# A first weight load issued in two parts, and the activations loaded as half rows, in a two-model decode attention kernel

## The chip, the cores and the metric

The kernel runs on one core of a Trainium2 chip. The metric is the device time of one execution in microseconds, the median of several runs. Profiles are of one execution, on the same core; its span runs from the first to the last instruction.

## The reference

Two independent attention blocks, A and B, each decode one token for 8 sequences. Each has its own x, K cache, V cache, wq and wo, and the two outputs are put side by side.

```python
B, Sq, D = 8, 1, 1024
H, Sk, Dh = 32, 4096, 128
q = (x @ wq).reshape(B, Sq, H, Dh).transpose(0, 2, 1, 3)
scores = einsum("bhqd,bhkd->bhqk", q, k_cache) * Dh ** -0.5
p = softmax(scores, axis=-1)
o = einsum("bhqk,bhkd->bhqd", p, v_cache)
out = o.transpose(0, 2, 1, 3).reshape(B, Sq, H * Dh) @ wo
```

All tensors are bf16. With one query per sequence, each byte of the caches is used once: K and V of both blocks, wq and wo come to 1,107 MB that must be read.

## The kernel before

**Tiles.** K and V are cut into tiles of one sequence and eight heads: 128 partitions (8 heads by 16 stretches of the key positions) of 64 KB each. There are 32 K tiles and 32 V tiles for each block, 64 pairs in all, numbered n = 0 to 63 (A first). The two wq and the two wo have the size of one such tile too.

**The ring.** All of them pass through `ring`, three slots of 64 KB on each partition (line 166). The `plan` (lines 237 to 241) fixes the order and the slot: wq of A into slot 1, K0 into slot 0, wq of B into slot 2, then K(n+1) into the slots 0 and 1 by turns and V(n) into slot 2. At the end come wo of A and of B. A load is issued when the last reader of the slot's tenant before is done (`load_tiles`, lines 257 to 275); `opUse` holds that last reader. Every load of the plan is issued by SyncE, in the plan's order, on SyncE's queue (queue 1 of the profile), so a load that waits holds up those behind it. Slot 2 has x as its first tenant (line 239): both x lie there (line 440) until they are transposed, so wq of B waits for the transposes.

**The x loads.** The two x (8 rows of 1,024 values, 2 KB a row) are issued by ScalarE on its own queue (queue 10), after `c_oh`, an early step on VectorE (line 441). `emit_xT` (lines 443 to 449) transposes them on PE: 16 transposes of 8 x 128 into PSUM tile `misc`, seen as bf16. VectorE copies them to `xT` (line 452). A column group of `xT` is 8 sequences of one of 8 chunks of D; the chunk k holds the rows p * 8 + k of wq, since wq is laid out with 8 consecutive rows on each partition.

**The q projection.** `make_q(c)` (lines 278 to 293) multiplies `xT` with wq of block c, 64 matmuls of 512 columns in two halves, and ScalarE copies the result to SBUF (L291). `make_qT` transposes it (L301 on PE, L305 on VectorE). `make_stage` (L312, ScalarE) and `make_qbc` (L317 PE, L319 ScalarE) spread the eight heads' q over the 128 partitions of a tile as `qbc`.

**The stages.** For each n, K tile n is worked in four chunks: VectorE multiplies with `qbc` (L330), adds halves (L335), PE adds up further in PSUM with identity matmuls (L345), VectorE reduces the rest (L353). Softmax's maximum, exponent and masks follow (L359 to L370); P times V of tile n - 1 runs on PE (L382) during the stage of tile n. Block B's q projection stands in tile 0's stage on PE, between the third and the fourth chunk's L345 (lines 471 to 474), and frees slot 2 for V0.

**The end.** After the last tile the sums are normalised and the wo products are made (L431). The output of each block is stored by SyncE (line 436); the store's DRAM side is written `"b (q n) -> q b n"` with q = 4, its SBUF side has 32 rows.

**Order of issue.** `P.run` writes each engine's instructions out in the order in which they were added, with a semaphore wait before an instruction where needed. SyncE's first two loads are issued ahead of the block in which the engines run side by side (line 507), the rest in it (line 512).

Of the kernel before, what the change touches and what calls it, by code (L numbers as in the profile page):

```python
# [31 lines left out]
class _Program:  # L32
# [11 lines left out]
    def add(self, eng, emit, deps=(), dma_key=None, moves=False):  # L44
        op = _Op(eng, emit, list(deps), dma_key, moves)
        if dma_key is not None:
            self.counts[dma_key] = self.counts.get(dma_key, 0) + 16
            op.token = (dma_key, self.counts[dma_key])
        for d in op.deps:
            if not (d.eng == "pe" and eng == "pe"):  # L50
                d.sig = True
        self.ops[eng].append(op)
        return op
# [86 lines left out]
def _build_kernel(nc, caches, out):  # L140
    B, Sq, D = caches[0][0].shape
    _, H, Sk, Dh = caches[0][1].shape
    NC = len(caches)
    assert B == 8 and Sq == 1 and Dh == 128 and Sk == 4096 and D == 1024 and H % 8 == 0 and 128 % H == 0
    DC = D // 128
# [16 lines left out]
    with es:  # L162
# [3 lines left out]
        ring = sb("ring", [128, 3, T * Dh], BF16)  # L166
        ident = sb("ident", [128, 128], BF16)
# [4 lines left out]
        xT = sb("xT", [128, NC * DC * B], BF16)  # L172
# [20 lines left out]
        misc = ps("misc")  # L193
        proj = ps("proj")
        q_ps = [o_ps, pv_ps]
        misc_bf16 = misc.bitcast(BF16)

        wo_cuts = ((0, 20), (20, H - 4), (H - 4, H - 1), (H - 1, H))
        sems = {e: es.enter_context(nc.semaphore(f"c_{e}")) for e in ENGINES[1:]}
# [4 lines left out]
        P = _Program()  # L204
        add = P.add

        def dma(out_ap, in_ap, key, deps, eng="sp"):
            return add(eng, lambda e: e.dma_start(out_ap, in_ap), deps, dma_key=key)
# [16 lines left out]
        c_oh = add("dve", lambda e: e.tensor_copy(own_h[:], own), [c_own])  # L225
# [5 lines left out]
        opT, opMul, opEacc, opRed, opNgm, opExp = {}, {}, {}, {}, {}, {}  # L231
# [18 lines left out]
        def where(n):  # L250

            return n // (B * HB), n // HB % B, n % HB

        def tile_of(kind, n):
            return ring[:, slot[(kind, n)], :]

        def load_tiles():
            while issued[0] < len(plan):
                kind, n, w = plan[issued[0]]
                prev = before[issued[0]]  # L260
                dep = opUse.get(prev)
                if prev is not None and dep is None:
                    return
                to, key = ring[:, w, :], ("t", w)
                if kind in ("k", "v"):
                    c, b, hb = where(n)
                    from_ = caches[c][1 if kind == "k" else 2][b, hb * HQ:(hb + 1) * HQ].rearrange("u (m t) d -> (u m) (t d)", m=MP)
                    opT[(kind, n)] = dma(to, from_, key, [dep])
                elif kind == "wq":
                    opT[(kind, n)] = dma(to[:, 0:DC * H * Dh], caches[n][3].rearrange("(p k) n -> p (k n)", k=DC), key, [dep])  # L270
                else:
                    from_ = caches[n][4].rearrange("(p r) n -> p (r n)", r=H)
                    for i, (r0, r1) in enumerate(wo_cuts if n == NC - 1 else ((0, H),)):
                        opT[(kind, n, i)] = dma(to[:, r0 * D:r1 * D], from_[:, r0 * D:r1 * D], key if n < NC - 1 else ("w", i), [dep])
                issued[0] += 1


        def make_q(c):
            w = tile_of("wq", c)
            for f in range(2):  # L280
                def emit(e, f=f):
                    for k in range(DC):
                        for hb in range(HB):
                            col = k * H * Dh + (2 * hb + f) * 512
                            i = e.matmul(q_ps[f][32 * hb:32 * hb + B, :], xT[:, (c * DC + k) * B:(c * DC + k + 1) * B],  # L285
                                         w[:, col:col + 512], start=(k == 0), stop=(k == DC - 1), tile_position=(0, 32 * hb))
                    return i
                opQ[(c, f)] = add("pe", emit, [c_xT, opT[("wq", c)]] + [opQs.get((c - 1, hb, f)) for hb in range(HB)])
                for hb in range(HB):
                    rows = slice(32 * hb, 32 * hb + B)  # L290
                    opQs[(c, hb, f)] = add("act", lambda e, rows=rows, f=f: e.activation(q_sb[rows, c, f * 512:(f + 1) * 512], q_ps[f][rows, :], ACTF.Copy),  # L291
                                           [opQ[(c, f)]])
            opUse[("wq", c)] = opQ[(c, 1)]
# [143 lines left out]
                            ("out", 0), [opEv[c]] if c == NC - 1 else [opEv[c], opT[("wo", NC - 1, len(wo_cuts) - 2)]], "sp"))  # L437


        x_sb = ring[0:B, 2, 0:NC * D].rearrange("p (c d) -> p c d", c=NC)  # L440
        op_x = [dma(x_sb[:, c, :], caches[c][0].rearrange("b s d -> b (s d)"), ("x", 0), [c_oh], "act") for c in range(NC)]

        def emit_xT(e):
            for c in range(NC):
                for k in range(DC):
                    col = (c * DC + k) * B
                    i = e.transpose(misc_bf16[:, col:col + B], x_sb[:, c, :].rearrange("b (p k) -> b k p", k=DC)[:, k, :],
                                    ident[0:B, 0:B])
            return i
        op_xT = opUse[("x", 0)] = add("pe", emit_xT, [c_ident, op_x[-1]])  # L450
        load_tiles()
        c_xT = add("dve", lambda e: e.tensor_copy(xT[:], misc_bf16[:, 0:NC * DC * B]), [op_xT])
        make_q(0)
        make_qT(0)
        make_stage(0)
# [3 lines left out]
        for n in range(NQ):  # L459
            P.mark(n)  # L460
            for r in range(NR):
                s = n * NR + r
                make_mul(s)
                if s >= LAG:
                    make_red(s - LAG)
                if r == LAG - 1 and n >= 1:
                    make_shift(n - 1)
                fold = make_fold(s)
                if r == LAG - 1 and n >= 1:
                    make_pm(n - 1)  # L470
                if n == 0 and r == NR - 1:
                    for c in range(1, NC):
                        make_q(c)
                        make_qT(c)
                if r == 2 and n >= 1:
                    make_pv(n - 1, 0, RG // 2)
                if r == 3 and n >= 1:
                    make_pv(n - 1, RG // 2, RG)
                    make_acc(n - 1)
                if r == 2 and n + 1 < NQ:  # L480
                    make_stage(n + 1)
                    make_qbc(n + 1)
                make_eacc(s, fold)
                load_tiles()
                if r == 3 and n >= 1:
                    make_ext(n - 1)
        P.mark(NQ)
        n = NQ - 1
# [4 lines left out]
        make_pv(n, 0, RG)  # L493
        make_acc(n)
        load_tiles()
        make_ext(n)
        make_norm(1)
# [6 lines left out]
            o.token = (("x", 0), 16 * NC)  # L504
        loops = {"pe": (1, 2, (NQ - 2) // 2), "dve": (3, 2, (NQ - 4) // 2), "act": (3, HB, (NQ - 4) // HB)}

        P.run("sp", nc.sync, sems, part=(0, 2))
        with nc.Block() as block:

            @block.sync  # L510
            def _(eng):
                P.run("sp", eng, sems, part=(2, None))

            @block.tensor
            def _(eng):
                P.run("pe", eng, sems, loops["pe"])

            @block.scalar
            def _(eng):
                P.run("act", eng, sems, loops["act"])  # L520

            @block.vector
            def _(eng):
                P.run("dve", eng, sems, loops["dve"])

            @block.gpsimd
            def _(eng):
                P.run("pool", eng, sems)
# [4 lines left out]
def bass_concat_heads__mha_block_cached__mha_block_cached__decode_kernel(  # L533
    nc, A_x, A_k_cache, A_v_cache, A_wq, A_wo, B_x, B_k_cache, B_v_cache, B_wq, B_wo, out,
):
    caches = [(A_x, A_k_cache, A_v_cache, A_wq, A_wo), (B_x, B_k_cache, B_v_cache, B_wq, B_wo)]
    _build_kernel(nc, caches, out)
# [28 lines left out]
```

## Time and profile before

| what | value |
|---|---|
| median of 3 runs | 2563.64 us (2563.33 to 2563.65) |
| span of the profiled execution | 2562.3 us |
| PE busy | 1115.7 us, 44% |
| VectorE (DVE) busy | 2170.6 us, 85% |
| ScalarE (ACT) busy | 129.9 us, 5% |
| queue 1 (SyncE's loads), share of 16 DMA engines | 99.9% |
| read from HBM | 1107.33 MB |

The median of the runs is 1.3 us above the profiled span, which leaves out what lies before the first and after the last instruction.

How to read the rows. A row of the timeline gives start, duration, engine, line, operation, the tile written and the tile read, and in brackets how long the engine was idle before and what ended that. PE is TensorE, DVE VectorE, ACT ScalarE, SP SyncE; a name with q (SPq, ACTq) is the engine's sequencer, which issues DMAs. A row of a DMA view gives packets, megabytes and the share of 16 DMA engines. A packet is one row of a transfer, or the 4-byte signal with which a DMA engine reports its part done; "under 512 B" counts such signals, and "under 2 KB" and "under 8 KB" include them. A view may be cut to a stretch of time; its 40 slices then divide that stretch. Packets are booked where they start.

### The profile page before, as it was taken

The numbers are of one execution on the slowest core, as the hardware profiler recorded it, in microseconds if no ns is written. First come the engines' busy times: TensorE is split into PE (matmuls) and PEld (weight loads), VectorE is DVE, ScalarE is ACT, GpSimd is POOL, SyncE is SP. The second block draws the span as 40 slices with busy tenths as digits, with TensorE's granted clock in tenths as the row PEclk, the third lists the DMA queues.
The fourth block names the chain that finished last, engine by engine and source line by source line (L and its number), as shares of the span: only waits on it lengthen the run. The fifth ranks groups of instructions, "written<-read, shape, count | busy, mean of one in ns | idle before, by whom it ended". The sixth has DMA issues, their size and how long they took to land.

```text
span 2562.3 us, 18832 instructions
## 1 busy us (share of the span) xinstructions
PE 1115.7 (44%) x7712; PEld 396.7 (15%) x7712; DVE 2170.6 (85%) x1042; ACT 129.9 (5%) x401; POOL 2.6 (0%) x15
## 2 busy tenths in 40 slices
PE   2443443443443443444444444434444434434434
PEld 1111111111111111111111111111111111111112
DVE  3898898898898898898898888988988988988983
ACT  1100000000000000000000000000000000000000
POOL 0000000000000000000000000000000000000000
PEclk7676766767767767766666766767667666767667
DMA  9999999999999999999999999999999999999999
GB/s 425 427 438 430 437 431 436 432 436 432 435 431 437 430 438 430 435 432 435 433 431 437 431 435 433 434 433 435 433 435 433 435 433 435 433 435 433 435 433 394
DMA packets 19554, 1107.51 MB, mean 432 GB/s; under 512 B 2184, under 2 KB 2248, under 8 KB 2520
## 3 DMA queue, kind: packets, MB, share of 16 engines
q1 hardware_dynamic: 19512, 1107.34, 99.9%
q8 instruction: 7, 0.11, 0.0%
q10 hardware_dynamic: 32, 0.03, 0.0%
q14 instruction: 3, 0.02, 0.0%
HBM read 1107.33 MB, written 0.03 MB: 432 GB/s over the span
## 4 chain that ended last, share of the span: by engine, by line
DMA 52%; DVE 28%; issue 16%; PE 4%; ACT 0%; another core or an unknown queue 0%; DVEq 0%; SPq 0%
DMA ring<-in_A_k_cache_dram 25%; DMA ring<-in_B_k_cache_dram 25%; DVE ring L330 10%; DVE ring L335 10%; PE red L345 4%; DVE s_sb L353 4%; DVE PM L370 3%; DMA ring<-in_B_wo_dram 2%; DVE rmax L359 1%; DVE rtmp L360 0%; ACT PM L291 0%; DVEq L135 0%; DVE ngm L363 0%; PE o L285 0%
## 5 line engine op out<-in xcount | busy, mean ns | idle before, releaser
L330 DVE TENSOR_TENSOR ring<-ring,qbc 128x8192 bf16<-128x8192 bf16 x256 | 1131.7, 4421 | 310.9 <-DMA ring<-in_A_k_cache_dram 158.0
L345 PE MATMUL red<-ring,ident 128*128 128x512 bf16 x2048 | 780.1, 550 | 1392.7 <-DVE ring L335 1392.7
L335 DVE TENSOR_TENSOR ring<-ring 128x4096 bf16<-128x4096 bf16 x256 | 582.3, 2274 | 0.0
L345 PEld LDWEIGHTS red<-ring,ident 128*128 128x128 bf16 x2048 | 238.5, 127 | 1842.6 <-DVE ring L335 1495.2
L353 DVE TENSOR_REDUCE s_sb<-red 128x64 f32<-128x1024 f32 x256 | 312.0, 1219 | 2.9 <-PE red L345 2.9
L382 PE MATMUL pv<-ring,PM 128*32 128x512 bf16 x4096 | 274.4, 415 | 4.6 <-DVE PM L370 4.6
L370 DVE TENSOR_TENSOR PM<-pe,own_h 128x2048 bf16<-128x2048 bf16 x64 | 146.2, 2284 | 0.7 <-ACT pe L365 0.7
L382 PEld LDWEIGHTS pv<-ring,PM 128*32 128x32 bf16 x4096 | 103.9, 104 | 188.4 <-issue 116.2
L319 ACT ACTIVATE qbc<-misc 128x128 bf16<-128x128 f32 x64 | 17.8, 278 | 1093.4 <-PE misc L317 1093.4
L365 ACT ACTIVATE pe<-s_sb,ngm 128x256 bf16<-128x256 f32 x64 | 32.5, 508 | 470.2 <-DVE ngm L363 470.2
L390 ACT ACTIVATE accS<-pv 128x512 bf16<-128x512 f32 x64 | 38.2, 597 | 350.5 <-PE pv L382 350.5
L399 PEld LDWEIGHTS o<-accS,E 128*32 128x32 bf16 x1024 | 31.3, 100 | 49.3 <-issue 48.1
L399 PE MATMUL o<-accS,E 128*32 128x32 bf16 x1024 | 38.1, 185 | 0.7 <-ACT accS L390 0.7
L405 ACT ACTIVATE o_sb<-o 32x32 f32 (+1 forms) x64 | 11.9, 186 | 449.5 <-PE o L399 448.9
L359 DVE TENSOR_REDUCE rmax<-s_sb 128x1 f32<-128x256 f32 x64 | 26.9, 420 | 2.2
L435 DVE CAST orow<-proj 128x256 bf16<-128x256 f32 x2 | 0.8, 424 | 28.7 <-PE proj L431 28.7
L431 PE MATMUL proj<-ring,on_sb 128*32 128x256 bf16 x256 | 12.1, 363 | 17.7 <-DMA ring<-in_A_wo_dram 9.9
L312 ACT ACTIVATE qst<-qT 128x128 bf16 (+1 forms) x64 | 18.7, 293 | 2.0 <-DVE qT L305 2.0
L305 DVE COPY qT<-misc 128x64 bf16<-128x64 bf16 x8 | 3.5, 436 | 17.6 <-PE misc L301 17.6
L360 DVE TENSOR_SCALAR rtmp<-half,rmax 128x32 f32<-128x32 f32 x64 | 15.4, 241 | 2.2
L363 DVE TRANSPOSE_TENSOR_REDUCE ngm<-rtmp 128x1 f32<-128x32 f32 x64 | 13.5, 211 | 2.2
L317 PE MATMUL misc<-ident,qst 128*128 128x128 bf16 x64 | 14.8, 232 | 0.9 <-ACT qst L312 0.9
(33 smaller groups left out, 65.5 us busy)
## 6 DMA issues: line engine op xcount, KB each, us to landing
ring<-in_B_wo_dram SPq DMA_DIRECT2D x1, 5120.0 KB, 33.6
ring<-in_B_wo_dram SPq DMA_DIRECT2D x1, 2048.0 KB, 38.2
ring<-in_B_wo_dram SPq DMA_DIRECT2D x1, 768.0 KB, 39.6
ring<-in_A_k_cache_dram SPq DMA_DIRECT2D x32, 40.0
ring<-in_A_v_cache_dram SPq DMA_DIRECT2D x32, 27.8
ring<-in_B_k_cache_dram SPq DMA_DIRECT2D x32, 39.8
ring<-in_B_v_cache_dram SPq DMA_DIRECT2D x32, 27.8
ring<-in_B_wo_dram SPq DMA_DIRECT2D x1, 256.0 KB, 39.7
```

Source lines behind the costliest of these rows:

```text
L312: return e.activation(qst[:, n % 2, :].rearrange("p (j m) -> p j m", m=MP), from_.unsqueeze(2).to_broadcast([128, HQ, MP]), ACTF.Copy)
L319: opQbc[n] = add("act", lambda e: e.activation(qbc[:, n % 2, :], misc[:, 0:Dh], ACTF.Copy), [opQb[n], _at(opMul, NR * (n - 2) + NR - 1)])
L330: opMul[s] = add("dve", lambda e: e.tensor_tensor(v, v, qbc[:, n % 2, :].unsqueeze(1).to_broadcast([128, CT, Dh]), ALU.mult), [opT[("k", n ...
L335: return add("dve", lambda e: e.tensor_tensor(v[:, :, 0:64], v[:, :, 0:64], v[:, :, 64:128], ALU.add), [opMul[s]])
L345: i = e.matmul(dst, ident[:], v[:, g, :, j, :], start=(j == 0), stop=(j == 3))
L353: opRed[s] = add("dve", lambda e: e.tensor_reduce(s_sb[:, n % 2, r * CT:(r + 1) * CT], red_ps[s % 2][:, :].rearrange("p (t w) -> p t w", w ...
L359: m = add("dve", lambda e: e.tensor_reduce(rmax[:], s_sb[:, n % 2, :], AX.X, ALU.max), [opRed[NR * n + NR - 1]])
L365: opExp[n] = add("act", lambda e, at: e.activation(pe[:], s_sb[:, n % 2, :], ACTF.Exp, bias=ngm[:, n % 2:n % 2 + 1], scale=scale, accum_ou ...
L370: opPM[n] = add("dve", lambda e: e.tensor_tensor(PM[:], pe[:].unsqueeze(2).to_broadcast([128, T, HQ]), own_h[:].unsqueeze(1).to_broadcast( ...
L382: i = e.matmul(pv_ps[32 * q:32 * (q + 1), :], PM[:, t:t + 4, :].rearrange("p t j -> p (t j)"), v[:, t * Dh:(t + 4) * Dh], start=(g == 0), ...
L390: opAcc[n] = add("act", lambda e: e.activation(accS[:], pv_ps[:], ACTF.Copy), [opPV[n], _at(opExt, n - 1)])
L399: x = e.matmul(to, E[:, i, PH - 1 - u:PH - 1 - u + MB], accS[:, i * 128 + H * u:i * 128 + H * (u + 1)], start=(i == 0 and u == 0), stop=(i ...
```

## The change

Three things are changed, and two follow from them.

1. The first load, wq of A, is issued as two DMAs: rows 0 to 15, then rows 16 to 127. Both count on the semaphore of slot 1; the q projection waits for the second's count. Three loads instead of two are now issued ahead of the block.
2. Each x is loaded as 16 half rows of 512 values: half 0 of the 8 sequences on 8 partitions, half 1 on the next 8. The two x take 32 partitions, the destination of each is 16 rows of 1 KB. The source is written with the half outermost.
3. The transposes become matmuls. For each chunk k and each half h, the 32 half rows (64 values of the chunk in each) are multiplied by the 16 columns of the identity that belong to that half; the result, 64 partitions by 16 columns (A's sequences, then B's), goes to partitions 64 h to 64 h + 63 of `misc`. There are 16 of these, with f32 results.
4. `xT` has the chunk outermost and the block inside it, and `make_q` reads it so.
5. The copy to `xT` reads `misc` as f32.

```diff
@@ load_tiles
                 elif kind == "wq":
-                    opT[(kind, n)] = dma(to[:, 0:DC * H * Dh], caches[n][3].rearrange("(p k) n -> p (k n)", k=DC), key, [dep])
+                    from_ = caches[n][3].rearrange("(p k) n -> p (k n)", k=DC)
+                    for p0, p1 in ((0, 16), (16, 128)) if n == 0 else ((0, 128),):
+                        opT[(kind, n)] = dma(to[p0:p1, 0:DC * H * Dh], from_[p0:p1, :], key, [dep])
@@ make_q
-                            i = e.matmul(q_ps[f][32 * hb:32 * hb + B, :], xT[:, (c * DC + k) * B:(c * DC + k + 1) * B],
+                            i = e.matmul(q_ps[f][32 * hb:32 * hb + B, :], xT[:, (k * NC + c) * B:(k * NC + c + 1) * B],
@@ after make_proj
-        x_sb = ring[0:B, 2, 0:NC * D].rearrange("p (c d) -> p c d", c=NC)
-        op_x = [dma(x_sb[:, c, :], caches[c][0].rearrange("b s d -> b (s d)"), ("x", 0), [c_oh], "act") for c in range(NC)]
+        x_sb = ring[0:NC * 2 * B, 2, 0:D // 2]
+        op_x = [dma(x_sb[2 * B * c:2 * B * (c + 1), :], caches[c][0].rearrange("b s (h e) -> h (b s) e", h=2), ("x", 0), [c_oh], "act")
+                for c in range(NC)]
 
         def emit_xT(e):
-            for c in range(NC):
-                for k in range(DC):
-                    col = (c * DC + k) * B
-                    i = e.transpose(misc_bf16[:, col:col + B], x_sb[:, c, :].rearrange("b (p k) -> b k p", k=DC)[:, k, :],
-                                    ident[0:B, 0:B])
+            mine = ident[0:2 * NC * B, 0:2 * NC * B].rearrange("p (c h b) -> p h c b", c=NC, h=2)
+            for k in range(DC):
+                for h in range(2):
+                    i = e.matmul(misc[64 * h:64 * (h + 1), k * NC * B:(k + 1) * NC * B].rearrange("p (c b) -> p c b", c=NC),
+                                 x_sb.rearrange("b (p k) -> b k p", k=DC)[:, k, :], mine[:, h], start=True, stop=True, tile_position=(0, 64 * h))
             return i
...
-        c_xT = add("dve", lambda e: e.tensor_copy(xT[:], misc_bf16[:, 0:NC * DC * B]), [op_xT])
+        c_xT = add("dve", lambda e: e.tensor_copy(xT[:], misc[:, 0:NC * DC * B]), [op_xT])
@@ the loads ahead of the block
-        P.run("sp", nc.sync, sems, part=(0, 2))
+        P.run("sp", nc.sync, sems, part=(0, 3))
...
-                P.run("sp", eng, sems, part=(2, None))
+                P.run("sp", eng, sems, part=(3, None))
```

## The prediction

> **What bounds the kernel now.** I read the page first, the mean rate and the row of DMA queues, to see which resource is never idle.
>
> ```profile
> span 2562.3 us, 18832 instructions
> DMA packets 19554, 1107.51 MB, mean 432 GB/s; under 512 B 2184, under 2 KB 2248, under 8 KB 2520
> q1 hardware_dynamic: 19512, 1107.34, 99.9%
> q10 hardware_dynamic: 32, 0.03, 0.0%
> ```
>
> Queue 1 is SyncE's. It keeps all 16 DMA engines at work for 99.9% of the span, at 432 GB/s. So the time is the bytes at that rate plus a start and an end; nothing done on a compute engine counts unless it makes queue 1 run dry. One 64 KB row on each of the 16 DMA engines is 1.049 MB, and at 432 GB/s takes 2.43 us (2.42 us below). A tile of 128 rows is eight such rows per DMA engine, 19.4 us. Queue 10 is ScalarE's: only the two x loads.
>
> Then the start, in order of time, for what SyncE issues and what each issue has waited for.
>
> ```profile
> 0.80 0.39 SPq L208 DMA_DIRECT2D ring<-in_A_wq_dram  x1
> 1.26 0.41 SPq L208 DMA_DIRECT2D ring<-in_A_k_cache_dram  x1
> 2.49 0.60 ACTq L208 DMA_DIRECT2D ring<-in_A_x_dram  x1
> 3.12 0.28 ACTq L208 DMA_DIRECT2D ring<-in_B_x_dram  x1
> 15.75 1.10 PE L447 MATMUL misc<-ident,ring 8*128 8x8 bf16 x16 [15.75 <-DMA ring<-in_B_x_dram]
> 16.89 0.33 SPq L208 DMA_DIRECT2D ring<-in_B_wq_dram  x1
> 16.89 0.23 DVE L452 COPY xT<-misc 128x128 bf16<-128x128 bf16 x1 [14.17 <-PE misc L447]
> 23.03 3.59 PE L285 MATMUL o<-ring,xT 128*8 128x512 bf16 x32 [6.17 <-DMA ring<-in_A_wq_dram]
> 29.25 0.33 SPq L208 DMA_DIRECT2D ring<-in_A_k_cache_dram  x1
> 34.33 0.28 ACT L319 ACTIVATE qbc<-misc 128x128 bf16<-128x128 f32 x1 [0.38 <-PE misc L317]
> 43.48 4.43 DVE L330 TENSOR_TENSOR ring<-ring,qbc 128x8192 bf16<-128x8192 bf16 x1 [9.87 <-DMA ring<-in_A_k_cache_dram]
> 72.76 0.33 SPq L208 DMA_DIRECT2D ring<-in_A_v_cache_dram  x1
> 80.93 0.33 SPq L208 DMA_DIRECT2D ring<-in_A_k_cache_dram  x1
> 82.18 4.42 DVE L330 TENSOR_TENSOR ring<-ring,qbc 128x8192 bf16<-128x8192 bf16 x1 [4.32 <-DMA ring<-in_A_k_cache_dram]
> ```
>
> SyncE issues in order: wq of A, K0, then wq of B, which waits until the transposes (L447) have freed ring slot 2, then K1, V0, K2. Until wq of B is issued, queue 1 holds just two tiles, 16 rows per DMA engine. **Everything hangs on when x lands**: now shortly before the transposes start at 15.75, with wq of B issued at 16.89, while those 16 rows last until about 41 us. The q projection then starts at 23.03, when wq of A is there, not when x is; its result (qbc) is ready at 34.61, 8.87 us before VectorE gets K0. So x has slack now. The question is whether the new x load keeps it.
>
> **How a small load gets through.** The packets in five stretches, one row time each after the first, in order: 0 to 7.2, 7.2 to 9.7, 9.7 to 12.1, 12.1 to 14.6 and 14.6 to 15.72 us.
>
> ```profile
> q1 hardware_dynamic: 32, 2.10, 77.0%
> ...
> DMA packets 24, 1.06 MB, mean 426 GB/s; under 512 B 0, under 2 KB 0, under 8 KB 8
> q10 hardware_dynamic: 8, 0.02, 1.7%
> ...
> DMA packets 24, 1.05 MB, mean 437 GB/s; under 512 B 8, under 2 KB 8, under 8 KB 8
> q10 hardware_dynamic: 8, 0.00, 0.2%
> ...
> DMA packets 24, 1.06 MB, mean 426 GB/s; under 512 B 0, under 2 KB 0, under 8 KB 8
> ...
> DMA packets 24, 1.05 MB, mean 936 GB/s; under 512 B 8, under 2 KB 8, under 8 KB 8
> ```
>
> In each of the last four, the DMA engines start 16 rows of queue 1 and 8 packets of queue 10: x of A (8 packets of 2 KB), its signals (8 packets under 512 B), x of B, its signals. All four were issued by 3.40 us, yet no two went back to back: **each packet of queue 10, even a 4-byte signal, waits for a 64 KB row of queue 1.** One turn costs 2.42 us. Today an x load of 8 rows has one row and one signal on each of 8 DMA engines, so both x take 4 turns.
>
> Over how many DMA engines is a load spread? The stretch 2560.2 to 2561.2 holds one output store, of 32 rows of 512 B; that from 15.72 to 41 us holds the signals of wq of A.
>
> ```profile
> DMA packets 36, 0.02 MB, mean 16 GB/s; under 512 B 4, under 2 KB 36, under 8 KB 36
> ...
> DMA packets 177, 10.50 MB, mean 415 GB/s; under 512 B 16, under 2 KB 16, under 8 KB 16
> ```
>
> A 128-row tile ends in 16 signals, x in 8, and the store in 4, though its SBUF side has 32 rows: its DRAM side is written "q b n" with q = 4 outermost. The spread follows the smaller outermost count.
>
> **The change, part by part.**
>
> *x over two DMA engines.* The new source is "h (b s) e" with h = 2 outermost, since the halves can't be merged with the rows; the destination has 16 rows. As with the store I take 2 DMA engines, each with 8 rows of 1 KB and a signal, so 9 packets per x and 18 for both, where there were 4. The other bound is 16 DMA engines, by the destination's rows, again 4 turns. The store is the same shape of access, so I take 2. [...]
>
> *When x lands then.* With a row between any two, 18 packets from about 7.3 us would need until 7.3 + 17 x 2.42 = 48.4 us. But queue 1 has only 16 rows per DMA engine: when they are gone the rest goes at once. The first rows of queue 1 start at about 1.9 us and end at about 5.1:
>
> ```profile
> GB/s 0 0 0 0 0 0 0 0 0 0 3641 1820 0 0 364 0 0 0 0 0 0 0 0 0 0 0 364 2185 1092 2185 0 0 0 0 0 0 0 0 0 0
> ```
>
> (the 40 slices of 0 to 7.2 us; bytes are booked where a packet starts, so the second rows start at 4.7 to 5.4). The 16th row ends at 5.1 + 15 x 2.42 = 41.4 us, plus 16 x rows at 0.04 us each (1 KB at the 27 GB/s of one DMA engine): x lands at **42.1 us**. Whether signals of queue 1 take a turn, or x begins one row earlier, doesn't move this; the end of queue 1 sets it.
>
> *First gap.* From the last signals (they stand in the stretch from 14.6 on) to PE's start at 15.75 are at most 1.15 us; I take the middle, 0.6. The transposes to the issue take 1.14 (15.75 to 16.89): wq of B is issued at 43.85. From an issue on idle DMA engines to the end of the first row were 4.3 us at the start (0.80 to 5.1). So wq of B's first row ends at 48.15, where it would have ended at 41.4 + 2.42 = 43.85 without a pause: **4.3 us lost**. If the restart takes 1.0 us plus a plain row of 2.42 (first bytes came 1.0 us after the first issue), it is 3.4.
>
> *Second gap.* xT is copied by 44.1 and the q projection starts at 44.15. From its start to qbc are 11.58 us (23.03 to 34.61), so VectorE starts K0 at 55.75, not 43.48: **12.3 us late**. V0 needs wq of B's slot, freed by B's q projection, which stands on PE behind three chunks of K0: it is issued at 72.76 + 12.3 = 85.05, and its first row ends at 89.35. Queue 1 with wq of B and K1 is dry at 48.15 + 15 x 2.42 = 84.45. V0's first row would have ended at 5.1 + 32 x 2.42 + 0.1 for the old x = 82.65 before. The two gaps together: 89.35 - 82.65 = **6.7 us**, 2.4 of it the second.
>
> *After that.* VectorE starts K1 at 82.18 - 4.32 + 12.3 = 90.2, 8.0 us late. The next V and K:
>
> ```profile
> 112.27 0.33 SPq L208 DMA_DIRECT2D ring<-in_A_v_cache_dram  x1
> 119.01 0.33 SPq L208 DMA_DIRECT2D ring<-in_A_k_cache_dram  x1
> 120.87 4.43 DVE L330 TENSOR_TENSOR ring<-ring,qbc 128x8192 bf16<-128x8192 bf16 x1 [4.78 <-DMA ring<-in_A_k_cache_dram]
> ```
>
> V1 is issued at about 120.3; queue 1 holds V0 and K2 until 89.35 + 15 x 2.42 = 125.7. Covered by 4 us after the restart's 1.0. VectorE is done with K1 at 116.09 + 8.0 = 124.1, before K2 lands, so it is back in step with the DMA, and the stages behind keep their margins.
>
> *The rest.* The load in 16 and 112 rows has one row and then seven per DMA engine, the same bytes: 16 signals more, of 4 bytes each, and one issue more on SyncE, 0.46 us ahead of K0, hidden by the 19 us of wq of A in the queue. The first row may start earlier because fewer rows are prepared (a gain of up to 0.3 us), or the second part may come late for it (a loss of as much): I take nothing. The 16 matmuls now contract 32 rows into 64 columns; the nearest row is the old 1.10 us, with 0.8 to 1.6 as bounds. The copy reads f32: the old 0.23 us to the mean of the final copies, twice as wide; I take 0.25.
>
> ```profile
> L435 DVE CAST orow<-proj 128x256 bf16<-128x256 f32 x2 | 0.8, 424 | 28.7 <-PE proj L431 28.7
> ```
>
> Both are on the path behind x, so ±0.5 us goes into the range. xT's new order of columns changes no instruction of the projection.
>
> **Sum.** I take 6.5 us, a little below 6.7 since the restart may be the shorter one. Span 2562.3 + 6.5 = 2568.8; the runs stand 1.3 us above the span (2563.64): **2570.1 us**, 0.25% slower.
>
> **The rivals.**
>
> *x lands early, nothing changes: 2563.5 us, chance 0.12.* Either x is spread over 16 DMA engines, or the 8 rows of one x share a turn. For the latter: no row of this trace has several small rows of one load beside a busy queue 1. Against it: a row and its signal, and the signal and the next x, never shared a turn. It decides from the number of turns: x must land by about 36 us (the K0 multiply may slip some 6 us before V0's issue comes after queue 1's end), so 12 turns or fewer. Then the time is that of before, less at most 0.3 us for the balance of the DMA engines, the not slower side. [...]
>
> *Only the first gap: 2567.5 us (3.4 to 4.3 lost), chance 0.06.* If the q chain runs faster from a late start, V0 comes in time. Nothing in the rows between 23.03 and 34.61 is waiting for DMA, so I give it little.
>
> *A third gap: 2573 to 2577 us, chance 0.04.* V1's margin is only 4 us. If VectorE runs later than reckoned, PV of tile 0 comes late and V1 leaves queue 1 dry too, each us late costing one, plus the restart.
>
> *Really faster, chance 0.02.* Queue 1 is at 99.9% now: there is no pause to remove, apart from 1 us at the start.
>
> **How the numbers follow.** The forecast has 0.76: 2568.8 to 2571.5 us. A difference under 0.2% (5.1 us) can't be told from none. Slower: 0.76 + 0.04 = 0.80. Same: 0.12 + 0.06 = 0.18. Faster: 0.02. The range 2566.5 to 2573.5 holds the forecast, the single gap and the low end of the third, and leaves out the early x.
>
> **What would show it.** Right: queue 10 with 32 rows and 4 signals (36 packets), spread from about 5 to 42 us; the transposes near 42.7; wq of B issued near 43.9; a hole in the DMA row between 41 and 45 and one near 85; the first K0 multiply near 55.8; VectorE waiting for K2 as before. Wrong: x landed by 20 us, or 16 signals per x, or a hole but no later V0.

## The result, and the profile after

The changed kernel takes 2590.85 us (median of 4 runs, 2590.32 to 2592.92); the kernel before took 2563.51 us beside it. The ratio is 1.0108, 95% interval 1.0096 to 1.012: 27.3 us slower, where 6.5 were forecast.

The head of the page and its rows of DMA queues:

```profile
span 2589.9 us, 18863 instructions
GB/s 271 396 435 435 436 429 433 435 436 432 429 436 435 435 426 435 435 436 431 432 433 437 431 431 435 435 433 429 435 435 435 430 434 433 436 432 431 435 435 394
q1 hardware_dynamic: 19528, 1107.34, 99.6%
q10 hardware_dynamic: 36, 0.03, 0.0%
```

The loss lies in the first two slices (65 us each): 271 and 396 GB/s, then 426 to 437 and a last slice of 394, as before. Queue 10 has 36 packets: 32 rows of x and 4 signals, so each x did go over two DMA engines. But the gap that was forecast for the first slice, 4.3 us of 65, can't bring it down to 271. The timeline of the start:

```profile
0.80 0.87 SPq L208 DMA_DIRECT2D ring<-in_A_wq_dram  x2
62.22 1.12 PE L450 MATMUL misc<-ident,ring 32*64 32x16 bf16 x16 [62.22 <-DMA ring<-in_B_x_dram]
63.37 0.35 SPq L208 DMA_DIRECT2D ring<-in_B_wq_dram  x1
63.73 3.58 PE L287 MATMUL o<-ring,xT 128*8 128x512 bf16 x32 [0.38 <-DVE xT L455]
75.71 4.42 DVE L332 TENSOR_TENSOR ring<-ring,qbc 128x8192 bf16<-128x8192 bf16 x1 [1.11 <-ACT qbc L321]
106.16 0.33 SPq L208 DMA_DIRECT2D ring<-in_A_v_cache_dram  x1
148.85 4.42 DVE L332 TENSOR_TENSOR ring<-ring,qbc 128x8192 bf16<-128x8192 bf16 x1 [3.88 <-DMA ring<-in_A_k_cache_dram]
```

The chain is the forecast one (transposes, then wq of B, then the q projection, then K0, then V0), but the transposes start at 62.22, not near 42.7. The table of stretches says why. A line gives a stretch and its length, the busy time of PE, of PE's weight loads, of VectorE, ScalarE and GpSimd with the number of instructions, the granted clock of PE, and in the last two columns the share of the 16 DMA engines and the rate in GB/s (a packet is booked where it starts, so a share can pass 1). First come two lines of the kernel before, for its first 64 KB row on each DMA engine and for eight later ones:

```profile
1.82:4.85 3.03, 0.00 (x0) 0.00 (x0) 0.41 (x3) 1.28 (x1) 1.68 (x8) 1.00 1.08 368
21.90:41.20 19.30, 7.84 (x97) 3.28 (x97) 1.74 (x4) 5.49 (x11) 0.00 (x0) 0.75 1.01 435
```

and these are of the changed kernel, for its first part of wq of A, its second, K0, and the two gaps:

```profile
1.85:11.20 9.35, 0.00 (x0) 0.00 (x0) 0.41 (x3) 1.28 (x1) 1.64 (x8) 1.00 1.47 217
11.20:41.00 29.80, 0.00 (x0) 0.00 (x0) 0.00 (x0) 0.00 (x0) 0.00 (x0) 1.00 0.89 227
41.00:60.50 19.50, 0.00 (x0) 0.00 (x0) 0.00 (x0) 0.00 (x0) 0.00 (x0) 1.00 0.95 404
60.50:65.00 4.50, 2.40 (x32) 1.48 (x36) 0.29 (x1) 0.00 (x0) 0.00 (x0) 1.00 0.67 234
103.00:108.00 5.00, 3.46 (x60) 1.36 (x52) 2.55 (x3) 3.44 (x6) 0.00 (x0) 0.93 0.62 210
```

Both gaps are there, near 62 and near 105. What the forecast did not have is the first 41 us. The DMA engines are busy all that time (0.89 and more), yet move half as much: the one row of each of them in the first part takes until 11.2 us, the seven rows of the second 30 us. (In the first stretch the second rows of most DMA engines are booked too, so its 217 GB/s is rather too high.) K0, in the same queue just behind, is back at about the usual rate. So the slowness goes with the two parts of wq of A.

Three theories were set against each other. **P**: the parts are slow at their destination, where the 16 rows of the first go to 16 neighbouring partitions. **S**: they are slow at their source, neighbouring rows in HBM. **X**: the small packets of x slow queue 1.

### The profile page after: what moved, and what is told of

It reads as the page before. It is cut to its first block, busy times and chain, and to the rows that moved or that the text cites. A ratio compares the mean times of both kernels' runs of the same rounds, so it can differ in the third digit from the quotient of the medians.

```text
span 2589.9 us, 18863 instructions
## 1 busy us (share of the span) xinstructions
PE 1122.8 (43%) x7712; PEld 397.8 (15%) x7712; DVE 2170.4 (84%) x1042; ACT 129.8 (5%) x401; POOL 2.6 (0%) x15
## 4 chain that ended last, share of the span: by engine, by line
DMA 49%; DVE 27%; issue 17%; PE 5%; another core or an unknown queue 2%; ACT 0%; DVEq 0%; SPq 0%
DMA ring<-in_B_k_cache_dram 25%; DMA ring<-in_A_k_cache_dram 23%; DVE ring L332 10%; DVE ring L337 10%; PE red L347 4%; DVE PM L372 3%; DVE s_sb L355 2%; DMA ring<-in_B_wo_dram 2%; DVE rmax L361 1%; DVE rtmp L362 0%; PE o L287 0%; ACT PM L293 0%; DVE qT L307 0%; PE pv L287 0%
```

## The experiments

**One part each.** The half rows of x without the split of wq. If all of the loss beyond the forecast came from the two parts of wq of A, the forecast's own times were to hold here: x at 42.1 us, V0's issue near 85, 2570.1 us in all (2568.5 to 2571.5).

```diff
-                    for p0, p1 in ((0, 16), (16, 128)) if n == 0 else ((0, 128),):
+                    for p0, p1 in ((0, 128),):
```

> The half rows of x are kept, wq of A is one load again. [...] Theory X (the many small packets of x on two DMA engines slow queue 1): the rows stay at 4 to 9 us, x lands near 60 us, time about 2590 us.

Measured: 2571.66 us, ratio 1.0032 (1.002 to 1.0045), 8.1 us slower than before. Its timeline, and the stretches of its two gaps:

```profile
43.32 1.12 PE L450 MATMUL misc<-ident,ring 32*64 32x16 bf16 x16 [43.32 <-DMA ring<-in_B_x_dram]
44.48 0.33 SPq L208 DMA_DIRECT2D ring<-in_B_wq_dram  x1
44.83 3.59 PE L287 MATMUL o<-ring,xT 128*8 128x512 bf16 x32 [0.39 <-DVE xT L455]
56.38 4.42 DVE L332 TENSOR_TENSOR ring<-ring,qbc 128x8192 bf16<-128x8192 bf16 x1 [1.11 <-ACT qbc L321]
86.43 0.33 SPq L208 DMA_DIRECT2D ring<-in_A_v_cache_dram  x1
...
42.50:45.40 2.90, 1.69 (x24) 1.31 (x28) 0.29 (x1) 0.00 (x0) 0.00 (x0) 1.00 0.00 1
85.60:87.40 1.80, 0.78 (x16) 0.15 (x8) 0.54 (x1) 1.73 (x4) 0.00 (x0) 1.00 0.23 73
```

Theory X falls: with the same packets of x, queue 1 runs at its usual rate (from 1.85 to 42.50 us 409 GB/s). The forecast's own picture is there: two holes in the DMA row (nothing for 2.9 us, then a share of 0.23 over 1.8 us), and each step within 1.4 us of its forecast time. The holes are narrower than the 8.1 us lost, because the first row after a pause is also slower than 2.42 us (in the kernel before, the first took from 1.82 to 4.85) and the DMA engines don't all stop at once. The time is 0.16 us above the range expected for this run.

The split of wq alone, x as before:

```diff
-                    opT[(kind, n)] = dma(to[:, 0:DC * H * Dh], caches[n][3].rearrange("(p k) n -> p (k n)", k=DC), key, [dep])
+                    from_ = caches[n][3].rearrange("(p k) n -> p (k n)", k=DC)
+                    for p0, p1 in ((0, 16), (16, 128)) if n == 0 else ((0, 128),):
+                        opT[(kind, n)] = dma(to[p0:p1, 0:DC * H * Dh], from_[p0:p1, :], key, [dep])
```

> x as in the kernel before, wq of A in 16 and 112 rows. Theory P, and likewise theory S (the rows are slow at their source in HBM, being neighbours there): the first part takes about 9 us, the second about 29, as in the changed kernel; K0 lands near 63 us instead of 43.5. x takes 4 turns and lands by 30 us, so wq of B is in the queue long before queue 1 is empty, and no gap follows. VectorE starts K0 when it lands, some 20 us late, and V0's issue moves by as much, with queue 1. Time 2563.5 + 20.5 = 2584 us (2582 to 2586). Theory X: 2563.5 us.

Measured: 2585.16 us, ratio 1.0084 (1.0067 to 1.0101), 21.6 us slower. Timeline and stretches:

```profile
29.34 1.10 PE L449 MATMUL misc<-ident,ring 8*128 8x8 bf16 x16 [29.34 <-DMA ring<-in_B_x_dram]
65.17 4.43 DVE L332 TENSOR_TENSOR ring<-ring,qbc 128x8192 bf16<-128x8192 bf16 x1 [10.05 <-DMA ring<-in_A_k_cache_dram]
95.59 0.33 SPq L208 DMA_DIRECT2D ring<-in_A_v_cache_dram  x1
...
1.85:11.20 9.35, 0.00 (x0) 0.00 (x0) 0.41 (x3) 1.28 (x1) 1.64 (x8) 1.00 1.34 196
11.20:41.00 29.80, 1.10 (x16) 1.05 (x16) 0.23 (x1) 0.00 (x0) 0.00 (x0) 1.00 0.90 219
```

The same two slow stretches, at 196 and 219 GB/s. x lands in time and there is no gap, so the loss is the slow load, handed on: VectorE gets K0 at 65.17 instead of 43.48, 21.7 us late, and the end is 21.6 us late. **The split is the larger part of the loss by far.** The parts alone add up to 29.7 us, and the changed kernel lost 27.3, so they overlap a little: on top of the half rows the split costs 2590.85 - 2571.66 = 19.2 us.

**Where the slow load is slow.** Six extra loads of 60 KB rows were put ahead of the kernel before, each waiting for the one in front of it:

```diff
+        op_pr = None
+        pr_from = [caches[c][3].rearrange("(p k) n -> p (k n)", k=DC) for c in range(NC)]
+        for i, (d0, d1, dstep, s0, s1, sstep) in enumerate(((0, 128, 1, 0, 128, 1), (0, 16, 1, 0, 16, 1), (0, 128, 8, 0, 16, 1),
+                                                            (0, 16, 1, 0, 128, 8), (0, 64, 1, 0, 64, 1), (16, 128, 1, 16, 128, 1))):
+            op_pr = dma(ring[d0:d1:dstep, 2, 2048:T * Dh], pr_from[i % 2][s0:s1:sstep, 2048:T * Dh], ("w", 0), [op_pr])
```

> The kernel before with six extra loads of wq rows (60 KB each) ahead of all others, into the part of ring slot 2 that x leaves free, each issued when the one before has landed; they only add time. In order: 128 rows to 128 partitions; 16 neighbouring rows to partitions 0 to 15; 16 neighbouring rows to every eighth partition; 16 rows, every eighth, to partitions 0 to 15; 64 rows to partitions 0 to 63; 112 rows to partitions 16 to 127. From issue to landing, with about 2.7 us of latency in each. [...] Theory S (the crowding is at the source rows in HBM): the third is as slow as the second (12), the fourth is fast (5), and 64 rows take about 12 us.

A latency of 2.7 us is what wq of A has in the kernel before: 22.1 us from issue to landing, less eight rows of 2.42.

The loads of this kernel in order of time; each is issued when the one above it has landed, so the differences of the first column are the times from issue to landing:

```profile
0.80 0.39 SPq L208 DMA_DIRECT2D ring<-in_A_wq_dram  x1
21.93 0.35 SPq L208 DMA_DIRECT2D ring<-in_B_wq_dram  x1
33.06 0.62 SPq L208 DMA_DIRECT2D ring<-in_A_wq_dram  x1
40.75 0.32 SPq L208 DMA_DIRECT2D ring<-in_B_wq_dram  x1
51.82 0.50 SPq L208 DMA_DIRECT2D ring<-in_A_wq_dram  x1
73.36 0.32 SPq L208 DMA_DIRECT2D ring<-in_B_wq_dram  x1
104.42 0.35 SPq L208 DMA_DIRECT2D ring<-in_A_wq_dram  x1
```

| load | source rows | partitions | issue to landing, us | expected by P | by S |
|---|---|---|---|---|---|
| 128 rows | 0 to 127 | 0 to 127 | 21.1 | 21 | 21 |
| 16 rows | 0 to 15 | 0 to 15 | 11.1 | 12 | 12 |
| 16 rows | 0 to 15 | every eighth | 7.7 | 7 | 12 |
| 16 rows | every eighth | 0 to 15 | 11.1 | 12 | 5 |
| 64 rows | 0 to 63 | 0 to 63 | 21.5 | 21 | 12 |
| 112 rows | 16 to 127 | 16 to 127 | 31.1 | 30 | |

The columns of P and S are the author's estimates; what P's 7 us and its 21 us for 64 rows rest on was not shown by any run before this one. Moving the destination apart makes 16 rows faster (7.7 us instead of 11.1); moving the source apart does nothing (11.1 again). Theory S falls: it is the destination that makes the load slow. Sixty-four rows take as long as 128 (21.5 and 21.1 us), and 112 rows take 10 us longer than 128 (31.1). The share of the 16 DMA engines in each stretch gives the time of one row (for 16 rows, share times stretch); here those of the second, third and fourth load:

```profile
q1 hardware_dynamic: 32, 0.98, 72.0%
q1 hardware_dynamic: 32, 0.98, 58.6%
q1 hardware_dynamic: 32, 0.98, 73.1%
```

That is 0.720 x 11.13 = 8.0 us, 0.586 x 7.69 = 4.5 and 0.731 x 11.07 = 8.1 us a row, where 60 KB take 2.3 in a 128-row load under way (2.42 for 64 KB). These loads have only a first row on each DMA engine, though, and a first row is slower in a 128-row load too. From 0 to 4.7 us, the stretch that holds the 16 first rows of the 128-row load:

```profile
q1 hardware_dynamic: 16, 0.98, 62.7%
```

That is 0.627 x 4.7 = 2.95 us a row, the number to set beside the 8.0 and the 4.5. They are 2.7 and 1.5 times as long. Why, these rows don't show.

A second set of loads tried more destinations, in the same code:

```diff
+        for i, (d0, d1, dstep, s0, s1, sstep) in enumerate(((0, 128, 1, 0, 128, 1), (0, 112, 7, 0, 16, 1), (0, 64, 4, 0, 16, 1),
+                                                            (0, 32, 2, 0, 16, 1), (56, 72, 1, 0, 16, 1), (0, 128, 8, 0, 128, 8))):
```

> Another six serial probe loads ahead of the kernel before, 60 KB rows. In order: 128 rows to 128 partitions; 16 neighbouring rows to every seventh partition (0 to 105), to every fourth of 0 to 63, to every second of 0 to 31, and to 56 to 71; last, 16 rows, every eighth, to every eighth partition. [...] So rows take 2.3 us for twelve of the second and 4.6 for the other four, 4.6 for all of the third, fourth and sixth, 9 for the fifth; from issue to landing 21, 7.7, 7.7, 7.7, 11.1 and 7.7 us. [...]

From issue to landing (differences of successive issues, as above): 21.1, 6.8, 7.2, 7.6, 11.1 and 7.7 us. The second and third load, the share of their stretches:

```profile
q1 hardware_dynamic: 32, 0.98, 61.6%
...
q1 hardware_dynamic: 32, 0.98, 63.1%
```

The fifth (16 neighbours, from 56 on) is as slow as those from 0 on (11.1 us), and every fourth of 0 to 63 is about as slow as every second of 0 to 31 (7.2 and 7.6 us). The sixth, with source and destination both spread, takes the same 7.7 us as the first set's load with only the destination spread. Every seventh partition has a mean row of 0.616 x 6.81 = 4.2 us, hardly under the 4.5 of the third (0.631 x 7.20). Nor is it the mixture of quick and slow rows that was expected. From 23.3 to 27.3 us all 16 rows start, the last within the first us, and no signal comes:

```profile
DMA packets 16, 0.98 MB, mean 246 GB/s; under 512 B 0, under 2 KB 0, under 8 KB 0
```

In the trace's records the 16 rows take 3.65 to 4.64 us, so none is as quick as a first row of the 128-row load (2.95). That was a miss: the 2.3 us for twelve rows and 4.6 for four were the author's estimate, and no run shows a ground for that division. So P holds as to the destination, and no more. What is shown: 16 neighbouring partitions are the slowest destination (8.0 us a row), 16 spread ones are quicker (4.2 to 4.6), all 128 quicker still (2.95 for the first row, 2.3 after it). Why 16 spread ones stay above 4 us is open; how the rows of a load that isn't 128 high are dealt to the DMA engines was not tried.

**The turns of x.** With x out of the ring, wq of B no longer waits for it, and queue 1 doesn't run dry while x is under way:

```diff
-        tenant = [None, None, ("x", 0)]
+        tenant = [None, None, None]
...
-        x_sb = ring[0:NC * 2 * B, 2, 0:D // 2]
+        x_sb = qT[0:NC * 2 * B].rearrange("p c n -> p (c n)")
```

(wq of A in one load, as in the first experiment.)

> As e1, and x lies in the buffer of qT instead of ring slot 2, so wq of B no longer waits for it. Theory of turns (each packet of x waits for one 64 KB row, 18 packets on each of two DMA engines): queue 1 doesn't run out, so x lands later than in e1, at 7.3 + 17 x 2.42 = 48.4 us; the q projection starts at about 50.4, VectorE starts K0 near 62, V0 is issued near 91 while queue 1 ends near 80: one gap instead of two, 91.3 + 4.3 - 82.7 = 12.9 us, time about 2576 us (2574 to 2578). If packets can share a turn: x lands by 42 us or sooner, and the time is 2570 us or less.

Measured: 2574.13 us, ratio 1.004 (1.0025 to 1.0054), 2.5 us slower than with x in the ring:

```profile
45.27 1.12 PE L450 MATMUL misc<-ident,qT 32*64 32x16 bf16 x16 [45.27 <-DMA qT<-in_B_x_dram]
89.28 0.33 SPq L208 DMA_DIRECT2D ring<-in_A_v_cache_dram  x1
...
81.70:90.20 8.50, 7.53 (x71) 2.39 (x69) 6.86 (x3) 2.54 (x5) 0.00 (x0) 0.70 0.00 0
```

One gap of 8.5 us, and none before it: taking the wait of wq of B away made the kernel slower, because more rows in queue 1 held x up longer. x landed about 4 us before the 48.4 forecast. Where that comes from is also seen with x in the ring (first experiment), in one row time, 22.1 to 24.5 us, in which queue 10 has 4 packets on its two DMA engines; in the changed kernel, 46.2 to 48.6 us, it has 2:

```profile
q10 hardware_dynamic: 4, 0.00, 0.5%
```

```profile
q10 hardware_dynamic: 2, 0.00, 0.2%
```

So a pair of packets shares a turn. In the trace's records it is the last two of the eight rows that each DMA engine has of an x: at 22.1 us in the first experiment, at 22.2 and again at 42.0 us in this one. One such pair for each x makes 16 turns instead of 18, and they account for it: 7.4 + 15 x 2.45 = 44.2 us. Why just these two share a turn is open.

In the three kernels in which V0 came late, the time is V0's issue and a constant: 2590.85 - 106.16 = 2484.7, 2571.66 - 86.43 = 2485.2, 2574.13 - 89.28 = 2484.9 us. **In these three, V0's issue sets the end.**

**The parts mended.** Half rows of x written so that 16 rows are outermost on both sides:

```diff
-caches[c][0].rearrange("b s (h e) -> h (b s) e", h=2)
+caches[c][0].rearrange("b s (h e) -> (b s h) e", h=2)
...
-rearrange("p (c h b) -> p h c b", c=NC, h=2)
+rearrange("p (c b h) -> p h c b", c=NC, h=2)
```

> wq of A in one load, and each x as 16 half rows with the sequence outermost and the half inside it, so that source and destination both count 16 rows; the identity's columns are picked accordingly. Theory P with the turns: 16 DMA engines and 16 signals per x, four turns again, x lands near 15 us and the time is that of before, 2563.5 us (2563.0 to 2564.2). If the half rows themselves or the matmuls cost something, it is over 2565 us.

Measured: 2564.01 us beside 2563.56, ratio 1.0001 (0.9992 to 1.001). Queue 10 has 64 packets now, 32 half rows and 32 signals, so each x goes over 16 DMA engines:

```profile
q10 hardware_dynamic: 64, 0.03, 0.0%
```

The half rows and the matmuls cost nothing beyond the interval; their spread over two DMA engines did (8.1 us in the first experiment).

wq of A cut by columns instead of rows, x as before:

```diff
+                    for k0, k1 in ((0, 1), (1, DC)) if n == 0 else ((0, DC),):
+                        opT[(kind, n)] = dma(to[:, k0 * H * Dh:k1 * H * Dh], from_[:, k0 * H * Dh:k1 * H * Dh], key, [dep])
```

> x as in the kernel before; wq of A in two loads, cut by columns instead of rows: one eighth of each of the 128 rows (8 KB), then the other seven (56 KB). Theory P: each part reaches all 128 partitions, so nothing crowds: 2563.5 us (2563.0 to 2564.5). If issuing the first load in two costs by itself (another issue, other signals, a later start of the second part): over 2565 us, and up to 2584 us.

Measured: 2563.22 us, ratio 0.9999 (0.999 to 1.0008). Two loads in place of one cost nothing; the cut across the partitions did (21.6 us).

Both together in the changed kernel:

> The changed kernel with both parts mended: wq of A cut by columns as in e5, the half rows of x ordered as in e4. Theory P: 2563.5 us (2563.0 to 2564.5); a gain over the kernel before of at most 0.5 us, since queue 1 had no gap to fill. If the two parts cost something together that neither costs alone, over 2565 us.

Measured: 2563.50 us, ratio 1.0 (0.9991 to 1.0009). Mended, the change does nothing either way. No version was found that is faster than the kernel before by more than these intervals.

## Why the prediction was wrong

**The step that failed** stands under "The rest": that the load in 16 and 112 rows has "one row and then seven per DMA engine, the same bytes". From there the prediction weighed only the signals, the one issue more and the start of each part, with bounds of 0.3 us (the first row started at 1.82 us in the kernel before and 0.03 us later in the changed one), and concluded "I take nothing". It counted bytes and packets for each DMA engine and took 2.42 us for each row, a duration measured on loads of 128 partitions; none of its rows showed a large load to fewer. With 16 or 112 partitions a row of 60 KB took 8.0 or some 4 us, and wq of A ended about 20 us late. None of the four rivals had this term either. The term is 21.6 us, measured alone, and it is all that the range missed: the first experiment's kernel, the change without the split, has 2571.66 us, inside the range of 2566.5 to 2573.5, though 0.2 us above the forecast's own 2568.8 to 2571.5. That the destination makes the load slow is shown, and that a cut by columns costs nothing; by what mechanism the partitions do it is open.

**x over two DMA engines** was right: 36 packets, 4 signals, as reckoned from the output store with its 4 signals; ordering the same rows so that 16 are outermost (64 packets, 32 of them signals) took the 8.1 us away.

**The turns** were right in kind and a little high in number: 18 forecast, 16 found. It made no difference to the forecast, since 16 turns still reach past the end of queue 1. The rival by which a whole x shares a turn falls; in the changed kernel, with queue 1 at its plain rate, each row time from 46.2 us on begins with one packet of x on each of two DMA engines.

**x lands when queue 1 runs dry**: right. The transposes were forecast at 42.7; they start at 43.32 without the split. With it the two tiles end near 61 us, and they start at 62.22.

**First gap, second gap**: both are there. V0's issue, forecast at 85.05, came at 86.43 without the split: 0.6 us from x and the transposes' start, and 0.8 between K0's start and V0's issue (30.05 us instead of 29.28). The reckoned 6.7 us and these two make 8.1, the time lost. The term was set at 6.5 for a shorter restart, which didn't come (wq of B was issued at 44.48, and by the trace's records its first rows ended at 48.6 to 49.3, 4.1 to 4.9 us later); it was too small by a fifth.

**After that**: right. V1 came in time and VectorE waits for K2 again (3.88 us idle at 148.85 in the changed kernel).

**The matmuls, the copy, xT's order**: right, nothing beyond the intervals in the mended kernels' times.

## What to carry to other kernels

Take a duration per row only for loads that spread over the partitions as the measured one did: here the first row of 60 KB on a DMA engine took 2.95 us in a load to 128 partitions and 8.0 in one to 16 neighbouring ones. If a large load has to be cut, cut it by columns and leave all 128 partitions in each piece (2563.22 us here, 2585.16 with the cut by rows). Beside a busy queue of large rows, count a small load in turns, not bytes: packets on each DMA engine times the time of one large row (here 16 turns of 2.45 us, after which the transposes started at 45.27), and look at which count stands outermost on both sides (here 2 gave two DMA engines and 16 gave 16). A load with slack of its own can still hold up the queue that waits for it (by 8.1 us in the first experiment), so ask what is left in that queue when it lands.

## What the runs showed of the hardware that was not expected

- A load to 64 neighbouring partitions took 21.5 us and one to all 128 took 21.1, with twice the bytes; 112 partitions took 31.1. The prediction had not reckoned with this; the estimate for theory P had, before that run.
- Sixteen rows to every seventh partition took 3.65 to 4.64 us each, where 2.3 had been expected for twelve of them.
- Block B's q projection, 64 matmuls, took 3.7 us in the kernel before and 4.4 us without the split of wq. The eighth column (the granted clock of PE) of the stretches in which it runs:

```profile
69.00:72.70 3.70, 3.70 (x65) 1.41 (x64) 3.70 (x3) 1.61 (x3) 0.00 (x0) 0.98 0.70 301
```

```profile
82.00:86.40 4.40, 4.38 (x65) 1.54 (x64) 4.13 (x3) 1.64 (x3) 0.00 (x0) 0.83 0.55 238
```

The granted clock was 0.98 in the one and 0.83 in the other. That is most of the 0.8 us by which V0's issue followed K0's start later than reckoned; why the clock was lower was not looked into.
